# Head of a fused layernorm, state-space and feed-forward kernel: immediate epsilon, column halves, other engines for two copies, one memset moved

## Chip, core, metric

The kernel runs on one core of a Trainium2 chip. The metric is the device time of one execution in microseconds. The engines are named as in the profile: PE (TensorE, matrix multiply; PEld is its weight load), DVE (VectorE), ACT (ScalarE), POOL (GpSimd), SP (SyncE). PSUM is the memory that TensorE writes, SBUF the one that all engines work from. DMAs are issued from queues of SP, ACT and POOL.

## What is computed

x has 2048 tokens of 512 columns, all in bf16. Layernorm without weights, then two branches on the normalized tokens, and a residual:

```python
xn = (x - mean(x)) / sqrt(var(x) + 1e-5)
# branch A: diagonal complex state-space scan over the 2048 tokens, 512 states
Bu = xn @ B_bar.T;  h[t] = Lam_bar * h[t-1] + Bu[t];  yA = 2 * real(h @ C.T) + xn * Dskip
# branch B: gated feed-forward, 1376 hidden columns
yB = (silu(xn @ w_gate) * (xn @ w_up)) @ w_down
out = x + yA + yB
```

## The kernel before

Tokens are cut into 16 tiles of 128 and four chunks of 512 (four tiles each). Tokens lie on partitions in `xall`; the matrix products need columns of x on partitions, so each normalized tile is transposed into `xnT`. The order of the work is written out by hand: each engine runs its instructions in the order in which the program issues them, and a list of VectorE work (`queue`, `pump`, `need`) is fed in between matmul groups by estimated costs. Every chunk goes through gate and up products (`gateup_tile`), the product with B (`bproj_tile`, line 357), rotation, scan and rotation back on VectorE (`rotation`, lines 367 to 381; `scan`, line 399), and the output products (`out_ffn`, `out_ssm`).

The change is in the head, chunk 0, which is handled tile by tile so that TensorE can start before the whole chunk is there:

- **Loads.** Line 123 loads tile 0 on SP's queue, line 125 tile 1 on ACT's. Line 124 clears half of tile 1's place just ahead of that, so ACT's load waits for a VectorE memset. Behind them come, alternately on SP and ACT, the first two columns groups of gate (line 126, 256 KB) and up (line 127, 256 KB), tiles 2 (SP) and 3 (ACT), and the next groups of gate and up (SP). POOL loads three parameter rows and builds the identity that the transposes need.
- **Dummies.** TensorE runs nine matmuls of 512 columns on constants at once (`dummy`, line 608), and four more of 128 columns behind the transposes of tile 0.
- **Layernorm of a tile.** VectorE takes statistics (`ln_stats`, lines 185 and 186; for tiles 1 and 3 written out, lines 638 and 653), ScalarE forms 1/sqrt(var + eps) as Ln and Exp (`rstd_act`, lines 190 and 191; the Ln reads eps from a column of biases, `eps_t`), VectorE normalizes in place (`norm_dve`, line 203). In VectorE's order the statistics of tile 1 (line 638) stand between those of tile 0 and the normalization of tile 0 (line 639).
- **Transposes.** `xT_pe` transposes a tile on TensorE in two halves of two column blocks (line 220) and copies each half from PSUM to `xnT`, on VectorE (line 227) or ScalarE (line 229). For tile 0 the first half is copied by VectorE, the second by ScalarE; for tile 1 both by ScalarE; for tiles 2 and 3 both by VectorE.
- **First matmuls.** `head_mm(which, lo, hi, ks, fis)` multiplies gate (0) or up (1), tiles lo to hi, column blocks ks, hidden blocks fis (line 631). Before, the order is: gate of tile 0, both transposes of tile 1, up of tile 0, then gate and up of tile 1, and so on.

Behind the head, `table_ops` builds a cosine table `c16` and a sine table `s16` on VectorE and ScalarE (`Sin`, line 284; the cosine of each half comes after the sine). `rotation` multiplies u by both: two products with its first part (f1 with the cosine, f2 with the sine), f3 (second part with the sine), their sum f4, f5 and f6.

Of the kernel before, what the change touches and what calls it, by code (L numbers as in the profile page):

```python
# [10 lines left out]
F32 = mybir.dt.float32  # L11
BF16 = mybir.dt.bfloat16
ALU = mybir.AluOpType
ACT = mybir.ActivationFunctionType
# [9 lines left out]
def kernel(  # L24
# [17 lines left out]
    nc = tc.nc  # L42
    _, L, D = A_x.shape
# [8 lines left out]
    KD = D // 128  # L52
    NQ = Pst // 128
    FT = (F + 127) // 128
# [4 lines left out]
    LA, LB = 32, 64  # L59
    FL = (FT - 1) * 128  # L60
    assert fsz[-1] == LA + LB and NCH % 2 == 0
    EPS = 1e-5

    const = ctx.enter_context(tc.tile_pool(name="const", bufs=1))
# [8 lines left out]
    def bank(shape=(128, CW), dtype=F32):  # L73
        return psum.tile(list(shape), dtype, name="ps")

    def flat(ap3):
        return ap3.rearrange("p q j -> p (q j)")
# [7 lines left out]
    xall = const.tile([128, NT, D], BF16, name="xall")  # L85
    xnT = const.tile([128, KD, L], BF16, name="xnT")
# [9 lines left out]
    wd_sb = const.tile([128, FT, D], BF16, name="wd_sb")  # L96
# [7 lines left out]
    def wslice(groups, fi, k):  # L104
        for (a, b), t in zip(fgroups, groups):
            if a <= fi < b:
                return t[:, k, (fi - a) * 128:(fi - a) * 128 + fsz[fi]]
# [6 lines left out]

    neg_half = const.tile([128, TPC], F32, name="neg_half")
    nc.vector.memset(neg_half[:], -0.5)
    eps_t = const.tile([128, 1], F32, name="eps_t")
    nc.vector.memset(eps_t[:], EPS)

    nc.scalar.preload_act_table_set("natural_log_exp_and_others")  # L120


    nc.sync.dma_start(out=xall[:, 0, :], in_=x_v[:, 0, :])
    nc.vector.memset(xall[:, 1, 0:D // 2], 0.0)
    nc.scalar.dma_start(out=xall[:, 1, :], in_=x_v[:, 1, :])
    load_w1(nc.sync, wg_g, wg_v, 0)
# [5 lines left out]
    prm_rows = const.tile([128, 128], BF16, name="prm_rows")  # L132
# [28 lines left out]
    ident = const.tile([128, 128], BF16, name="ident")  # L161
# [4 lines left out]


    gu_last = [const.tile([128, CW], BF16, name=f"gu_last{i}") for i in range(3)]
    for t in (*(g[LB + LA:128, :] for g in gu_last), wd_sb[LB + LA:128, FT - 1, :]):
        nc.vector.memset(t, 0.0)  # L170


    stats = const.tile([128, NT, 6], F32, name="stats")
    mv = const.tile([128, NT, 2], F32, name="mv")
    ve = const.tile([128, NT], F32, name="ve")
# [5 lines left out]
    def xn_tile(c):  # L181
        return xn_end if c == NCH - 1 else xall[:, c * TPC:(c + 1) * TPC, :]

    def ln_stats(n):
        nc.vector.bn_stats(out=stats[:, n, :], in_=xall[:, n, :])  # L185
        nc.vector.bn_aggr(out=mv[:, n, :], in_=stats[:, n, :])

    def rstd_act(n):

        nc.scalar.activation(out=ve[:, n:n + 1], in_=mv[:, n, 1:2], func=ACT.Ln, bias=eps_t[:, 0:1])  # L190
        nc.scalar.activation(out=rstd[:, n:n + 1], in_=ve[:, n:n + 1], func=ACT.Exp, scale=-0.5)

    def ln_rstd(a, b):
# [4 lines left out]
        nc.vector.scalar_tensor_tensor(out=nb[:, a:b], in0=mv[:, a:b, 0], scalar=-1.0, in1=rstd[:, a:b],  # L198
                                       op0=ALU.mult, op1=ALU.mult)

    def norm_dve(n):
        c, i = divmod(n, TPC)
        nc.vector.tensor_scalar(out=xn_tile(c)[:, i, :], in0=xall[:, n, :], scalar1=mv[:, n, 0:1],
                                scalar2=rstd[:, n:n + 1], op0=ALU.subtract, op1=ALU.mult)

    def norm_act(n):
# [3 lines left out]

    HK = KD // 2

    def xT_pe(n, on_dve=(), prm_too=False):

        c, i = divmod(n, TPC)
        for h in range(2):
            tp = bank((128, HK * 128 + 128), BF16)
            for k in range(HK):
                lo = (h * HK + k) * 128
                nc.tensor.transpose(out=tp[:, k * 128:(k + 1) * 128], in_=xn_tile(c)[:, i, lo:lo + 128],  # L220
                                    identity=ident[:])
            if prm_too and h == 1:
                prm_transpose(tp[:, HK * 128:])
            dst = xnT[:, h * HK:(h + 1) * HK, n * 128:(n + 1) * 128]
            src = tp[:, 0:HK * 128].rearrange("p (k t) -> p k t", k=HK)
            if h in on_dve:
                nc.vector.tensor_copy(out=dst, in_=src)
            else:
                nc.scalar.copy(out=dst, in_=src)
        return tp[:, HK * 128:]  # L230

    def xT_dma(n):
# [12 lines left out]
    c2re, nc2re, nc2im = sm("c2re", NQ), sm("nc2re", NQ), sm("nc2im", NQ)  # L245
    kk, fs1, fc1 = sm("kk", 2, NQ), sm("fs1", 2, NQ), sm("fc1", 2, NQ)
    V = nc.vector

    def prm_transpose(pp):
        nc.tensor.transpose(out=pp, in_=prm_rows[:], identity=ident[:])  # L250

    def params_a(pp):
        V.tensor_copy(out=prm[:].rearrange("p t q -> p (t q)"), in_=pp[:, 0:3 * NQ])
# [107 lines left out]
    def rotation(src, dst, back):  # L361

        box = {}

        def mul(i, tab):
            t = ssm.tile([128, W], BF16, name="pm", bufs=3)
            V.tensor_tensor(out=t[:], in0=flat(src()[:, i]), in1=flat(tab[:]), op=ALU.mult)  # L367
            return t

        def f1():  # L370
            box[0] = mul(0, c16)
        def f2():
            box[1] = mul(0, s16)
        def f3():
            box[2] = mul(1, s16)
        def f4():
            V.tensor_tensor(out=flat(dst()[:, 0]), in0=box[0][:], in1=box[2][:], op=ALU.subtract if back else ALU.add)
        def f5():
            box[3] = mul(1, c16)
        def f6():  # L380
            V.tensor_tensor(out=flat(dst()[:, 1]), in0=box[3][:], in1=box[1][:], op=ALU.add if back else ALU.subtract)
        return [(1.15, f) for f in (f1, f2, f3, f4, f5, f6)]

    def ssm_ops(c):

# [6 lines left out]


        ops = rotation(lambda: u_tiles[c], lambda: u_tiles[c], False)
        for q in range(NQ):
            for part in range(2):
# [20 lines left out]
        def wt():  # L417
            if c not in w_tiles:
                w_tiles[c] = ssm.tile([128, 2, NQ, CW], BF16, name="wt", bufs=2)
            return w_tiles[c]  # L420
        back = rotation(g, wt, True)
        return ops, back

# [182 lines left out]
    def dummy(n, cols):  # L606
        for _ in range(n):
            nc.tensor.matmul(warm[:, 0:cols], lhsT=ones[:, 0:128], rhs=ones[:, 0:cols], start=True, stop=True)  # L608

    def ln_rest(c, on_act):  # L610
        ops = [(0.7, lambda n=n: ln_stats(n)) for n in range(c * TPC, (c + 1) * TPC)]
        def fin():
            ln_rstd(c * TPC, (c + 1) * TPC)
        def nbf():
            ln_nb(c * TPC, (c + 1) * TPC)
        ops += [(0.1, fin)]
        tail = [(0.1, nbf)] if on_act else []
        for n in range(c * TPC, (c + 1) * TPC):
            def one(n=n):
                (norm_act if on_act else norm_dve)(n)  # L620
                xT_dma(n)
            tail.append((0.05 if on_act else 0.35, one))
        return ops, tail
# [3 lines left out]
    def head_mm(which, lo, hi, ks, fis):  # L627

        for fi in fis:
            for k in ks:  # L630
                nc.tensor.matmul(held[fi][which][:, lo * 128:hi * 128], lhsT=wslice((wg_g, wu_g)[which], fi, k),  # L631
                                 rhs=xnT[:, k, lo * 128:hi * 128], start=(k == 0), stop=(k == KD - 1))

    allk = range(KD)
    dummy(9, CW)
    ln_stats(0)
    rstd_act(0)
    nc.vector.bn_stats(out=stats[:, 1, :], in_=xall[:, 1, :])
    norm_dve(0)
    nc.vector.bn_aggr(out=mv[:, 1, :], in_=stats[:, 1, :])  # L640
    rstd_act(1)
    xT_pe(0, on_dve=(0,))
    dummy(4, 128)
    norm_dve(1)
    ln_stats(2)

    head_mm(0, 0, 1, range(0, HK), (0, 1))
    head_mm(0, 0, 1, range(HK, KD), (0, 1))
    xT_pe(1)
    rstd_act(2)  # L650
    head_mm(1, 0, 1, range(0, HK), (0, 1))
    head_mm(1, 0, 1, range(HK, KD), (0, 1))
    nc.vector.bn_stats(out=stats[:, 3, :], in_=xall[:, 3, :])
    norm_dve(2)
    nc.vector.bn_aggr(out=mv[:, 3, :], in_=stats[:, 3, :])
# [3 lines left out]
    head_mm(0, 1, 2, range(HK, KD), (0, 1))  # L659
    head_mm(1, 1, 2, range(HK, KD), (0, 1))  # L660
    head_mm(0, 0, 2, allk, (2,))
    pp = xT_pe(2, on_dve=(0, 1), prm_too=True)
    head_mm(1, 0, 2, allk, (2,))
    norm_dve(3)
    params_a(pp)
    params_a2()
    head_mm(0, 2, 3, range(0, HK), range(H))
    head_mm(1, 2, 3, range(0, HK), range(H))
    xT_pe(3, on_dve=(0, 1))
    head_mm(0, 2, 3, range(HK, KD), range(H))  # L670
    head_mm(1, 2, 3, range(HK, KD), range(H))
    params_sin()
# [145 lines left out]
```

## Time and profile before

| | us |
|---|---|
| median of three runs | 179.19 |
| lowest and highest | 179.1, 179.68 |
| span of the profiled execution, first to last instruction | 177.3 |

The profiled execution is known by its span; the median of the runs is 1.9 us above it, which is what lies around the span.

| engine | busy us | share of the span |
|---|---|---|
| PE | 172.9 | 97% |
| DVE | 154.4 | 87% |
| ACT | 94.7 | 53% |
| POOL | 23.2 | 13% |

A group in the profile is a line, an engine, an operation and `out<-in`. A matmul's busy time overlaps its neighbours', since matmuls are pipelined: the distance of two starts says what one costs. `[0.44 <-DMA ...]` is idle time of the engine before the group and what ended it. The chain of work that ended last goes back from the last instruction to what released each step. The DMA view of a window names each queue with its packets in that window: q1 is SP's, q10 ACT's, q0 POOL's.

### The profile page before, as it was taken

Reading aid. Unit: us, or ns where it says so; the run is one execution under the profiler, and the core shown is the slowest. Engines: PE = TensorE matmul, PEld = TensorE weight load, DVE = VectorE, ACT = ScalarE, POOL = GpSimd, SP = SyncE. Lnnn points to the kernel's source line nnn. Section 1 sums busy time; section 2 is a strip of 40 time slices with the busy share of each in tenths; the row PEclk is TensorE's granted clock in tenths of the full one; section 3 lists DMA queues with packets and bytes.
Section 4 is the critical chain, followed back from the end, with each engine's and each line's share of the span. In section 5 each row is a group of like instructions: output and inputs, shape, how many; then the busy total and the mean of one; then the engine's idle time right before and its main releaser. Section 6 shows DMA issues by size and latency. Waiting matters only on the chain.

```text
span 177.3 us, 2449 instructions
## 1 busy us (share of the span) xinstructions
PE 172.9 (97%) x900; PEld 83.6 (47%) x916; DVE 154.4 (87%) x238; ACT 94.7 (53%) x173; POOL 23.2 (13%) x29
## 2 busy tenths in 40 slices
PE   8999999999999999999999999999999999999993
PEld 2884444444444444444444444444444444444743
DVE  6789997999999977899999999999999999990033
ACT  4589696977499369914966662013766600220000
POOL 6003000001200140000700000014280000150000
DMA  5999749973041024900440000005469500072012
GB/s 163 316 264 239 148 90 261 334 126 89 0 96 26 0 52 96 355 0 0 60 62 2 0 0 4 0 0 61 58 97 177 86 0 0 0 85 33 4 50 69
DMA packets 29131, 15.53 MB, mean 88 GB/s; under 512 B 18848, under 2 KB 29056, under 8 KB 29088
## 3 DMA queue, kind: packets, MB, share of 16 engines
q1 hardware_dynamic: 24416, 11.41, 28.8%
q0 software_dynamic: 3456, 3.28, 13.7%
q10 hardware_dynamic: 1248, 0.69, 1.3%
q8 instruction: 7, 0.11, 0.3%
q14 instruction: 4, 0.03, 0.1%
HBM read 8.03 MB, written 5.24 MB: 75 GB/s over the span
## 4 chain that ended last, share of the span: by engine, by line
PE 98%; issue 1%; DVE 0%
PE ps L432 36%; PE ps L528 19%; PE ps L545 16%; PE ps L357 16%; PE ps L631 3%; PE ps L608 2%; PE ps L483 2%; PE ps L535 2%; PE ps L472 1%; PE ps L220 1%; DVE res L548 0%; PE ps L250 0%
## 5 line engine op out<-in xcount | busy, mean ns | idle before, releaser
L432 PE MATMUL ps<-xnT,wg 128*128 128x512 bf16 x144 | 37.8, 379 | 0.4
L432 PE MATMUL ps<-xnT,wu 128*128 128x512 bf16 x145 | 37.3, 379 | 0.0
L528 PE MATMUL ps<-wd_sb,guT 128*128 128x512 bf16 (+2 forms) x177 | 36.7, 355 | 0.2
L399 DVE TENSOR_TENSOR_SCAN g<-r_t,car,u 128x512 bf16<-128x512 f32 x24 | 28.8, 1264 | 0.0
L545 PE MATMUL ps<-CF,wt 128*128 128x512 bf16 (+2 forms) x141 | 28.2, 355 | 0.2
L357 PE MATMUL ps<-xnT,BT 128*128 128x512 bf16 x126 | 28.2, 379 | 0.1
L446 ACT ACTIVATE guT<-ps 128x512 bf16<-128x512 f32 x40 | 24.6, 615 | 5.0 <-PE ps L432 5.0
L447 ACT CAST u<-ps 128x512 bf16<-128x512 f32 x40 | 24.1, 602 | 5.2 <-PE ps L432 5.1
L528 PEld LDWEIGHTS <-guT 128*128 128x128 bf16 x180 | 16.9, 98 | 18.0
L432 PEld LDWEIGHTS <-wu 128*128 128x128 bf16 x148 | 14.5, 98 | 17.5
L432 PEld LDWEIGHTS <-wg 128*128 128x128 bf16 x148 | 14.4, 98 | 17.2
L555 ACT CAST res<-ps 128x512 bf16<-128x512 f32 x12 | 6.7, 594 | 28.1 <-PE ps L545 28.1
L556 POOL DMA_DIRECT2D out_dram<-res x12 | 10.5, 1041 | 78.0 <-ACT res L555 78.0
L545 PEld LDWEIGHTS <-wt 128*128 128x128 bf16 x144 | 13.4, 98 | 14.4 <-issue 0.4
L357 PEld LDWEIGHTS <-BT 128*128 128x128 bf16 x128 | 12.5, 98 | 15.1
L359 ACT CAST u<-ps 128x512 bf16<-128x512 f32 x32 | 17.6, 588 | 3.7 <-PE ps L357 3.6
L451 DVE TENSOR_TENSOR guT<-guT,u 128x1024 bf16<-128x1024 bf16 x20 | 13.5, 680 | 0.0
L548 DVE TENSOR_TENSOR res<-ps,xn_end 128x512 bf16<-128x512 f32 (+2 forms) x6 | 3.0, 514 | 11.8 <-PE ps L545 11.8
L195 POOL TENSOR_TENSOR rstd<-ve,neg_half 128x4 f32<-128x4 f32 x3 | 5.3, 1761 | 53.9 <-DVE ve L194 53.9
L367 DVE TENSOR_TENSOR pm<-u,c 128x2048 bf16<-128x2048 bf16 x8 | 9.8, 1221 | 1.2 <-ACT c L284 1.1
L185 DVE BATCH_NORM_STATS2 stats<-xall 128x6 f32<-128x512 bf16 x14 | 9.5, 676 | 0.4 <-DMA xall<-in_A_x_dram 0.4
L367 DVE TENSOR_TENSOR pm<-g,c 128x2048 bf16<-128x2048 bf16 x8 | 9.7, 1215 | 0.1
(108 smaller groups left out, 166.6 us busy)
## 6 DMA issues: line engine op xcount, KB each, us to landing
out_dram<-in_A_x_dram SPq DMA_DIRECT2D x1, 1536.0 KB, 7.0
out_dram<-res POOLq DMA_DIRECT2D x12, 128.0 KB, 3.0
out_dram<-xall POOLq DMA_DIRECT2D x3, 512.0 KB, 7.6
wd_sb<-in_B_w_down_dram SPq DMA_DIRECT2D x1, 1280.0 KB, 10.9
xall<-in_A_x_dram SPq DMA_DIRECT2D x1, 1024.0 KB, 6.1
xall<-in_A_x_dram SPq DMA_DIRECT2D x2, 256.0 KB, 4.6
wg<-in_B_w_gate_dram SPq DMA_DIRECT2D x1, 512.0 KB, 5.6
wu<-in_B_w_up_dram SPq DMA_DIRECT2D x1, 512.0 KB, 6.1
```

Of the source, the lines that this page charges most:

```text
L185: nc.vector.bn_stats(out=stats[:, n, :], in_=xall[:, n, :])
L357: nc.tensor.matmul(ps[:], lhsT=BT[:, part, k, q * 128:(q + 1) * 128], rhs=xnT[:, k, c * CW:(c + 1) * CW], start=(k == 0), stop=(k == KD - 1))
L359: nc.scalar.copy(out=u_tiles[c][:, part, q, :], in_=ps[:])
L367: V.tensor_tensor(out=t[:], in0=flat(src()[:, i]), in1=flat(tab[:]), op=ALU.mult)
L399: V.tensor_tensor_scan(out=g()[:, part, q, :], data0=r_t[:, q:q + 1].to_broadcast([128, CW]), data1=u_tiles[c][:, part, q, :], initial=ini ...
L432: nc.tensor.matmul(ps[:fs, lo:hi], lhsT=wslice(groups, fi, k), rhs=xnT[:, k, c * CW + lo:c * CW + hi], start=(k == 0), stop=(k == KD - 1))
L446: nc.scalar.activation(out=guT[:fs, fi, :], in_=psg[:fs], func=ACT.Silu)
L447: nc.scalar.copy(out=u_pair[c][:fs, fi % 2, :], in_=psu[:fs])
L451: products.append(lambda: V.tensor_tensor(out=g, in0=g, in1=u, op=ALU.mult))
L528: nc.tensor.matmul(o[:], lhsT=gu_tiles[c][:, fi, i * 128:(i + 1) * 128], rhs=wd_sb[:, fi, lo:hi], start=(fi == 0), stop=False)
L545: nc.tensor.matmul(o[:], lhsT=w_tiles[c][:, part, q, i * 128:(i + 1) * 128], rhs=CF[:, part, q, lo:hi], start=False, stop=(c > 0 and part ...
L556: nc.gpsimd.dma_start(out=out_v[:, n, :], in_=res[:], accum_op=ALU.add)
```

## The change

- The Ln takes epsilon as an immediate; `eps_t` and its memset are gone.
- The memset of `wd_sb`'s unused rows moves from the end of the memsets to before the memset of tile 1's place (and so before ACT's first load).
- `norm_dve` can take a range of columns; tiles 0 and 1 are normalized in two halves.
- `xT_pe` handles one half. For tile 0 VectorE copies both halves, and one of the four short dummies stands between the halves. For tile 1 the first half of up of tile 0 stands between the two halves, its second half behind them; `rstd_act(2)` comes after that.
- In the forward rotation the two sine products f2 and f3 come ahead of the cosine product f1; the rotation back keeps its order.
- The calls for tiles 2 and 3 are written for the new form of `xT_pe` and do what they did.

```diff
-    eps_t = const.tile([128, 1], F32, name="eps_t")
-    nc.vector.memset(eps_t[:], EPS)
...
     nc.sync.dma_start(out=xall[:, 0, :], in_=x_v[:, 0, :])
+    nc.vector.memset(wd_sb[LB + LA:128, FT - 1, 0:D], 0.0)
     nc.vector.memset(xall[:, 1, 0:D // 2], 0.0)
     nc.scalar.dma_start(out=xall[:, 1, :], in_=x_v[:, 1, :])
...
-    for t in (*(g[LB + LA:128, :] for g in gu_last), wd_sb[LB + LA:128, FT - 1, :]):
-        nc.vector.memset(t, 0.0)
+    for g in gu_last:
+        nc.vector.memset(g[LB + LA:128, :], 0.0)
...
-        nc.scalar.activation(out=ve[:, n:n + 1], in_=mv[:, n, 1:2], func=ACT.Ln, bias=eps_t[:, 0:1])
+        nc.scalar.activation(out=ve[:, n:n + 1], in_=mv[:, n, 1:2], func=ACT.Ln, bias=EPS)
...
-    def norm_dve(n):
+    def norm_dve(n, lo=0, hi=D):
         c, i = divmod(n, TPC)
-        nc.vector.tensor_scalar(out=xn_tile(c)[:, i, :], in0=xall[:, n, :], scalar1=mv[:, n, 0:1],
+        nc.vector.tensor_scalar(out=xn_tile(c)[:, i, lo:hi], in0=xall[:, n, lo:hi], scalar1=mv[:, n, 0:1],
...
-    def xT_pe(n, on_dve=(), prm_too=False):
+    def xT_pe(n, h, on_dve, prm_too=False):
...
-        return [(1.15, f) for f in (f1, f2, f3, f4, f5, f6)]
+        return [(1.15, f) for f in ((f1, f2, f3, f4, f5, f6) if back else (f2, f3, f1, f4, f5, f6))]
...
-    norm_dve(0)
+    norm_dve(0, 0, DH)
+    norm_dve(0, DH, D)
     nc.vector.bn_aggr(out=mv[:, 1, :], in_=stats[:, 1, :])
     rstd_act(1)
-    xT_pe(0, on_dve=(0,))
-    dummy(4, 128)
-    norm_dve(1)
+    xT_pe(0, 0, True)
+    dummy(1, 128)
+    xT_pe(0, 1, True)
+    dummy(3, 128)
+    norm_dve(1, 0, DH)
+    norm_dve(1, DH, D)
     ln_stats(2)
-
-    head_mm(0, 0, 1, range(0, HK), (0, 1))
-    head_mm(0, 0, 1, range(HK, KD), (0, 1))
-    xT_pe(1)
+    head_mm(0, 0, 1, kh[0], (0, 1))
+    head_mm(0, 0, 1, kh[1], (0, 1))
+    xT_pe(1, 0, False)
+    head_mm(1, 0, 1, kh[0], (0, 1))
+    xT_pe(1, 1, False)
+    head_mm(1, 0, 1, kh[1], (0, 1))
     rstd_act(2)
-    head_mm(1, 0, 1, range(0, HK), (0, 1))
-    head_mm(1, 0, 1, range(HK, KD), (0, 1))
```

More of the change, by code (lines that the diff above doesn't have):

```diff
@@ L211 @@
     HK = KD // 2
-    def xT_pe(n, on_dve=(), prm_too=False):
+    def xT_pe(n, h, on_dve, prm_too=False):
         c, i = divmod(n, TPC)
[L216 to L229, printed above, removed]
+        tp = bank((128, HK * 128 + 128), BF16)
+        for k in range(HK):
+            lo = (h * HK + k) * 128
+            nc.tensor.transpose(out=tp[:, k * 128:(k + 1) * 128], in_=xn_tile(c)[:, i, lo:lo + 128], identity=ident[:])
+        if prm_too:
+            nc.tensor.transpose(out=tp[:, HK * 128:], in_=prm_rows[:], identity=ident[:])
+        dst = xnT[:, h * HK:(h + 1) * HK, n * 128:(n + 1) * 128]
+        src = tp[:, 0:HK * 128].rearrange("p (k t) -> p k t", k=HK)
+        if on_dve:
+            nc.vector.tensor_copy(out=dst, in_=src)
+        else:
+            nc.scalar.copy(out=dst, in_=src)
         return tp[:, HK * 128:]
@@ L247 @@
     V = nc.vector
-    def prm_transpose(pp):
-        nc.tensor.transpose(out=pp, in_=prm_rows[:], identity=ident[:])
     def params_a(pp):
@@ L634 @@
     allk = range(KD)
+    kh = (range(0, HK), range(HK, KD))
+    DH = D // 2
     dummy(9, CW)
@@ L661 @@
     head_mm(0, 0, 2, allk, (2,))
-    pp = xT_pe(2, on_dve=(0, 1), prm_too=True)
+    xT_pe(2, 0, True)
+    pp = xT_pe(2, 1, True, True)
     head_mm(1, 0, 2, allk, (2,))
@@ L668 @@
     head_mm(1, 2, 3, range(0, HK), range(H))
-    xT_pe(3, on_dve=(0, 1))
+    xT_pe(3, 0, True)
+    xT_pe(3, 1, True)
     head_mm(0, 2, 3, range(HK, KD), range(H))
```

## The prediction

> **What bounds the kernel now.** I read the chain of work that ended last first, then the timelines of the first 12 us, engine by engine, then the DMA views of short windows. The page says where the time goes:
>
> ```profile
> span 177.3 us, 2449 instructions
> ...
> PE 98%; issue 1%; DVE 0%
> ```
>
> TensorE is the chain, nearly without a break. The list of TensorE's waits agrees: its own queue names one, 0.8 us at the launch, and its weight loads name one on another engine, 0.9 us on line 203. After 12 us, weight loads and matmuls wait for nobody. So only two things move the end: how early the useful work of TensorE starts, and how dense it is until about 12 us. The stretch in question (timeline, TensorE; columns: start us, busy us, then the group):
>
> ```profile
> 3.72 1.06 PE L608 MATMUL ps<-const-bfloat16-1.0 128*128 128x512 bf16 x2
> 4.76 0.61 PE L220 MATMUL ps<-ident,xall 128*128 128x128 bf16 x4
> 5.16 0.50 PE L608 MATMUL ps<-const-bfloat16-1.0 128*128 128x128 bf16 x4
> 5.54 0.67 PE L631 MATMUL ps<-xnT,wg 128*128 128x128 bf16 x8
> 6.05 0.39 PE L220 MATMUL ps<-ident,xall 128*128 128x128 bf16 x4
> 6.27 0.61 PE L631 MATMUL ps<-xnT,wu 128*128 128x128 bf16 x8
> 6.79 0.38 PE L631 MATMUL ps<-xnT,wg 128*128 128x128 bf16 x4
> ```
>
> The nine wide dummies start 0.427 us apart, the last at 4.15, so their slots end at 4.57; the transposes of tile 0 begin at 4.76. Between 4.57 and 7 us TensorE stands still for about 0.19 (normalization), 0.04, 0.07 and 0.07 us (copies of transposes): 0.37 us in all, and no edit of this head can win more. What feeds it (timeline, VectorE):
>
> ```profile
> 0.84 0.06 DVE L118 MEMSET eps_t<- 128x1 f32 x1
> 0.90 0.17 DVE L124 MEMSET xall<- 128x128 uint32 x1
> ...
> 2.07 0.27 DVE L170 MEMSET wd_sb<- 32x256 uint32 x1
> 2.78 0.69 DVE L185 BATCH_NORM_STATS2 stats<-xall 128x6 f32<-128x512 bf16 x1 [0.44 <-DMA xall<-in_A_x_dram]
> 3.51 0.18 DVE L186 BATCH_NORM_AGGREGATE mv<-stats 128x2 f32<-128x6 f32 x1
> 3.61 0.66 DVE L638 BATCH_NORM_STATS2 stats<-xall 128x6 f32<-128x512 bf16 x1
> 4.29 0.41 DVE L203 TENSOR_SCALAR xall<-xall,mv,rstd 128x512 bf16<-128x512 bf16 x1
> ```
>
> The statistics of tile 1 (line 638) stand ahead of tile 0's normalization (line 203), and end at 4.27, just as ScalarE has tile 0's 1/sqrt ready (4.26). Whatever delays tile 1's data delays tile 0.
>
> **The change, part by part, if every load kept its place.** These are the gains.
>
> Ln with an immediate: it takes 0.29 us, the Exp beside it, which reads no column of biases, 0.20. I take 0.09 (bounds 0 and 0.09). Tile 0's 1/sqrt is ready at 4.16.
>
> Normalization in halves: a 128x512 takes 0.41; in the run of four on line 203 at 17.97 to 19.35 starts are 0.32 apart, and the 128x4 operations of lines 296 and 329 follow one another at 0.07 to 0.08. So about 0.25 of the 0.32 scales with columns: a half starts 0.19 after the one before and takes 0.28 (bounds 0.16, a 128x4 row, and 0.41, the whole). The first half would end at 4.20 + 0.28 = 4.48 instead of 4.70; but the dummies hold TensorE until 4.57, so of 0.22 only 0.19 arrive.
>
> VectorE copies both halves of tile 0 (0.29 each, against 0.37 on ScalarE): the second half is there at 5.64 instead of 5.78. What is late next is tile 1: its normalization now stands behind two copies and ends 0.2 later (6.03 against 5.81); ScalarE's copies of tile 1 follow. That up's first half stands between tile 1's two transposes hides most of it. Following it through, the first tile-1 matmul (6.79 before) comes at 6.65: a gain of 0.13, which then persists, as TensorE is dense from there on. The moved dummies cost nothing: there are four as before.
>
> Sine table first: VectorE waited 1.12 us at 28.6 for the cosine (line 284). The sine multiply can start at 28.6, but the next one needs the last cast of u, which ends at 30.15 behind the cosine on ScalarE; I count 0.7 us of VectorE time won, and nothing at the end, since TensorE doesn't wait for VectorE there. Were that cover gone, it would be worth 0.7. In later chunks u is ready long before: chunk 1's casts end at 39.3 and its rotation starts at 74.8.
>
> **What the moved memset does to the queues.** VectorE clears wd_sb (0.27) before the memset of tile 1 instead of eps_t (a slot of 0.05), so the tile-1 memset ends 0.22 later. ScalarE's queue waits for just that memset with its first load, and two more are behind it; SP's queue is not held:
>
> ```profile
> 1.10 0.41 ACTq L125 DMA_DIRECT2D xall<-in_A_x_dram  x1
> 1.53 0.46 ACTq L112 DMA_DIRECT2D wu<-in_B_w_up_dram  x1
> 2.02 0.53 ACTq L129 DMA_DIRECT2D xall<-in_A_x_dram  x1
> ```
>
> ```profile
> 0.74 0.40 SPq L123 DMA_DIRECT2D xall<-in_A_x_dram  x1
> 1.20 0.42 SPq L112 DMA_DIRECT2D wg<-in_B_w_gate_dram  x1
> 1.66 0.51 SPq L128 DMA_DIRECT2D xall<-in_A_x_dram  x1
> ```
>
> Tile 1's load goes out at 1.32 instead of 1.10, and so behind gate's first 256 KB (1.20); up's weights at 1.75, behind tile 2 (1.66); tile 3 at 2.24, beside gate's second group (2.21). Does the order matter? The DMA views of short windows say that large loads move one after another. Between 2.9 and 3.5 us, though up's load on q10 had been issued at 1.53, only q1 moved; between 3.9 and 4.3 only q10 (and two packets of q0), though tile 2 on q1 had been issued at 1.66:
>
> ```profile
> q1 hardware_dynamic: 281, 0.14, 86.4%
> ```
>
> ```profile
> q10 hardware_dynamic: 220, 0.11, 104.5%
> ```
>
> Gate's 256 KB hold the engines for about 1.05 us, from their first packets (2.55) to up's first (3.60). If they go ahead, tile 1 lands not at 1.10 + 2.0 = 3.1 but at about 4.15 (bounds: 3.33, its own delay of 0.22 alone; 4.4, the order of packets as bad as the 1.3 us that gate's load took to its last packet).
>
> Then: tile-1 statistics start at 4.19 instead of 3.61 and end at 4.85; the first half of tile 0's normalization, next in VectorE's queue, runs from 4.77 to 5.05; the transposes start at 5.10, 0.34 later than before, and TensorE idles 0.53 after its dummies. The copy comes 0.43 after that, as before (5.53 to 5.82); the first gate matmuls start at 5.88, the second four at 6.10. Tile 1 is normalized from 5.95 to 6.42, its transposes run at 6.32 and 6.65, ScalarE's copy (0.37) ends at 7.00, and the first tile-1 matmul starts at 7.05 against 6.79: **0.27 later than before**. Half of the delay is absorbed by the halves and the earlier second copy.
>
> What stands behind: up's weights, landed at 5.73 before, are needed at 6.43, which I cost at nothing. Tile 3 landed at 6.2. If gate's second group passes it (its 128 KB moved for about 1.1 us), it lands at 7.3, just what its statistics need before they hold up tile 2's normalization; I take 0.04 for this, bounds 0 and 0.35. The parameter rows and the identity on GpSimd come 0.22 later and keep over 0.4 us of slack (identity at 3.75 before).
>
> **Sum.** 0.27 + 0.04 = 0.31 us on a span of 177.3, so 177.6. Outside the span the change moves nothing; the median of the shown runs lies 1.9 above it, so 179.19 + 0.31 = **179.5**.
>
> **Rivals.**
> The loads keep their order (179.06). Up to 3.6 us the trace also fits a strict turn between the two queues, SP, ACT, SP, ACT: then tile 1 still goes second and lands at 3.34, before 3.61, and the gain of 0.13 stands, bounds 0.37 (every idle stretch gone) and a loss of 0.08 (halves as slow as wholes, 0.41). [...]
>
> The clock (slower, about 181). TensorE starts at half rate: 128-column starts are 0.107 apart until 5.38 and 0.056 after 5.54, 4.6 us after its first dummy. If a 0.53 us hole made it begin again, counted from 5.1 it would be fast only at 9.7; at most (9.7 - 5.4)/2 = 2.1 us on top of the 0.3, some 1.5 where it waits anyway. It decides if the hole is too long for whatever watches activity; the 0.19 us hole of before was not. [...]
>
> That the Ln or the halves save nothing changes little: in the forecast the Ln is hidden behind the statistics, halves at full price add 0.13.
>
> **How the numbers follow.** The order flips and costs 0.3: 0.52 (of it 0.19 beyond 0.54 us, if tile 3 or the halves add their bounds). The order holds: 0.35 (0.10 of it faster by over 0.54, which takes more than the idle I can see). The clock: 0.13. 0.3% of 179.19 is 0.54 us, about what a measurement of this kernel can tell from no change. So faster 0.10, same 0.25 + 0.33 = 0.58, slower 0.19 + 0.13 = 0.32. Range: below, the order holds with nearly all idle gone and the scatter of the runs, 178.7; above, 179.19 + 0.27 + 0.35 + 0.13 = 179.9 and some scatter, 180.1. It leaves out the clock and the extreme gains.
>
> **What would show it.** Right: VectorE's wait for tile 1 ahead of line 638's statistics, near 0.6 us; the first transposes at 5.1; TensorE without waits after 8 us. Wrong: those statistics at 3.6 and transposes at 4.57 (the order held); 128-column starts 0.107 apart after 5.6 us (the clock); any TensorE wait after 12 us, which I exclude.

## The result, and the profile after

The changed kernel takes **180.37 us** (median of six runs, 180.22 to 181.76) against 179.19: a ratio of 1.0082, 95% interval 1.0054 to 1.0111. Forecast were 179.5 us, in a range up to 180.1, so the loss came out nearly four times as large as forecast (1.18 us instead of 0.31). The six runs fall into two groups: four at 180.22 to 180.39 and two at 181.69 and 181.76. The profiled one is of the second group:

```profile
span 179.9 us, 2470 instructions
...
PE 95%; DMA 2%; ACT 0%; DVE 0%; issue 0%
```

TensorE is still the chain, but a load now has 2% of it. The head of the changed kernel in the timeline of all engines (start us, busy us, engine, line, group; idle time and its end in brackets):

```profile
0.97 0.27 DVE L122 MEMSET wd_sb<- 32x256 uint32 x1
1.20 0.42 SPq L112 DMA_DIRECT2D wg<-in_B_w_gate_dram  x1
1.31 0.17 DVE L123 MEMSET xall<- 128x128 uint32 x1
1.51 0.41 ACTq L124 DMA_DIRECT2D xall<-in_A_x_dram  x1
...
5.01 0.69 DVE L634 BATCH_NORM_STATS2 stats<-xall 128x6 f32<-128x512 bf16 x1 [1.12 <-DMA xall<-in_A_x_dram]
5.62 0.59 DVE L202 TENSOR_SCALAR xall<-xall,mv,rstd 128x256 bf16<-128x256 bf16 x2
6.01 0.39 PE L218 MATMUL ps<-ident,xall 128*128 128x128 bf16 x2 [1.23 <-DVE xall L202]
...
6.83 1.06 PE L625 MATMUL ps<-xnT,wg 128*128 128x128 bf16 x8
...
8.97 0.63 PE L625 MATMUL ps<-xnT,wg 128*128 128x128 bf16 x4
```

Read it from the top. The moved memset runs first, tile 1's load waits for the memset behind it and goes out at 1.51 (1.10 before), now behind gate's (1.20). Its data are there at 4.99 (3.12 before): VectorE stands still for 1.12 us ahead of tile 1's statistics. Tile 0's normalization, next in its queue, starts at 5.62 and the transposes at 6.01 (4.76 before), after TensorE has idled 1.23 us. The first matmul of tile 1 comes at 8.97 instead of 6.79.

One row more is needed to read that last number. Weight loads of the first matmuls, from the view of this line between 6 and 9.7 us (min, median and max in ns, then first and last start):

```profile
L625 PEld LDWEIGHTS <-wg x12: 151/151/151, 6.7 to 9.2; 128*128 128x128 bf16 x12
```

They take 151 ns each until 9.7 us and 97 behind it, and matmuls start 0.107 us apart instead of 0.056: TensorE's clock is at half rate until about 9.8 us, where by the distance of the starts it was released at 5.4 in the profile of before. That is what divides the two groups of runs, as far as the experiments can show it (one execution of each kernel has a profile).

So two things were lost: about 1.1 us in every run, by the load, and 1.4 us more in some, by the clock. The 0.13 us that the other edits were to bring isn't seen. One thing went as foreseen without moving the end: at 32.77 us VectorE waits 0.46 us for the cast of u, where it waited 1.12 for the cosine table.

### The profile page after: what moved, and what is told of

Its sections match the earlier page's. It is cut to its first block, busy times and chain, and to the rows that moved or that the text cites. A ratio compares the mean times of both kernels' runs of the same rounds, so it can differ in the third digit from the quotient of the medians.

```text
span 179.9 us, 2470 instructions
## 1 busy us (share of the span) xinstructions
PE 175.1 (97%) x916; PEld 85.0 (47%) x916; DVE 155.0 (86%) x240; ACT 94.5 (53%) x172; POOL 23.3 (13%) x29
## 4 chain that ended last, share of the span: by engine, by line
PE 95%; DMA 2%; ACT 0%; DVE 0%; issue 0%
PE ps L426 36%; PE ps L522 19%; PE ps L539 15%; PE ps L351 15%; PE ps L625 4%; DMA xall<-in_A_x_dram 2%; PE ps L529 2%; PE ps L477 2%; PE ps L466 1%; PE ps L218 1%; ACT L118 0%; PE ps L602 0%; DVE xall L202 0%; DVE res L542 0%; PE ps L220 0%
## 5 line engine op out<-in xcount | busy, mean ns | idle before, releaser
L426 PE MATMUL ps<-xnT,wu 128*128 128x512 bf16 x148 | 38.0, 379 | 0.0
L361 DVE TENSOR_TENSOR pm<-u,s 128x2048 bf16<-128x2048 bf16 x8 | 9.5, 1219 | 0.5 <-ACT u L353 0.5
```

The source lines that it names most:

```text
L426: nc.tensor.matmul(ps[:fs, lo:hi], lhsT=wslice(groups, fi, k), rhs=xnT[:, k, c * CW + lo:c * CW + hi], start=(k == 0), stop=(k == KD - 1))
```

## The experiments

All were timed beside runs of the kernel before on the same chip (medians 179.18 to 179.32). Times are us; "issued" and "landed" are those of tile 1's load in the profiled execution (landed is when the last of its 16 parts was reported), "tile 1" is the start of the first gate matmul of tile 1, "clock" when TensorE's granted clock goes up to full rate by the record in the kept trace (before and e7 have no such record; there it is when matmuls of 128 columns begin to start 0.056 apart).

| kernel | median (range, runs) | ratio, 95% interval | issued | landed | tile 1 | clock | span |
|---|---|---|---|---|---|---|---|
| before | 179.19 | | 1.10 | 3.12 | 6.79 | 5.4 | 177.3 |
| changed | 180.37 (180.22 to 181.76, 6) | 1.0082, 1.0054 to 1.0111 | 1.51 | 4.99 | 8.97 | 9.8 | 179.9 |
| e1 memset back | 179.28 (179.05 to 179.73, 11) | 1.0001, 0.9992 to 1.0009 | 1.07 | 3.21 | 6.93 | 6.0 | 177.5 |
| e2 memset alone | 180.85 (180.09 to 181.82, 6) | 1.0090, 1.006 to 1.012 | 1.51 | 5.05 | 8.00 | 4.1 | 178.6 |
| e3 twelve dummies | 180.34 (180.07 to 180.45, 5) | 1.0059, 1.0047 to 1.0071 | 1.51 | 5.03 | 8.00 | 3.7 | 178.5 |
| e4 load held | 180.95 (180.08 to 181.87, 6) | 1.0107, 1.0075 to 1.0139 | 1.46 | 4.78 | 7.75 | 4.2 | 178.3 |
| e5 tile 2 held | 181.23 (180.09 to 181.65, 6) | 1.0099, 1.0072 to 1.0126 | 1.51 | 4.71 | 8.69 | 9.9 | 179.8 |
| e6 statistics later | 180.53 (180.44 to 180.67, 5) | 1.0074, 1.0062 to 1.0086 | 1.51 | 5.01 | 8.21 | 5.1 | 178.8 |
| e7 whole tiles | 179.40 (179.12 to 179.8, 12) | 1.0012, 1.0004 to 1.002 | 1.07 | 3.48 | 7.51 | 6.3 | 178.0 |
| e8 six dummies | 180.60 (179.19 to 181.35, 12) | 1.0063, 1.0038 to 1.0088 | 1.09 | 3.35 | 7.90 | 10.1 | 179.6 |
| e9 gate held too | 180.08 (180.01 to 180.34, 6) | 1.0044, 1.0032 to 1.0056 | 1.50 | 4.82 | 7.78 | 4.8 | 178.3 |
| e10 sine first alone | 179.28 (178.97 to 179.77, 12) | 0.9999, 0.9988 to 1.0011 | 1.09 | 3.25 | 7.31 | 6.5 | 177.9 |
| e11 gate held longer | 181.12 (180.09 to 181.97, 6) | 1.0107, 1.0073 to 1.014 | 1.50 | 3.81 | 7.83 | 4.6 | 178.4 |
| e12 tile 1 on SP | 179.77 (179.46 to 180.19, 8) | 1.0026, 1.0015 to 1.0038 | 1.20 | 3.24 | 7.39 | 4.3 | 178.1 |

Compare the columns "tile 1" and "span": where the clock is at full rate by then, each adds to its value of before what the other does, to 0.2 us (e2 1.21 and 1.3; e12 0.60 and 0.8; e1 0.14 and 0.2). A delay of tile 1's first matmul goes to the end in full. The changed kernel's 2.18 becomes 2.6, as eight more matmuls start 0.05 late each before the clock is released.

### Is it the memset? (e1, e2)

e1 is the changed kernel with the moved memset back at its old place, e2 the kernel before with nothing but that move (and `eps_t`'s memset behind it, out of its way).

```diff
# e1, against the changed kernel
-    nc.vector.memset(wd_sb[LB + LA:128, FT - 1, 0:D], 0.0)
     nc.vector.memset(xall[:, 1, 0:D // 2], 0.0)
...
     for g in gu_last:
         nc.vector.memset(g[LB + LA:128, :], 0.0)
+    nc.vector.memset(wd_sb[LB + LA:128, FT - 1, 0:D], 0.0)
```

> The changed kernel with the memset of wd_sb's rows back behind the other memsets; all other edits stay. Queue theory (the moved memset lets ACT's first load fall behind gate's, and tile 1's statistics hold up tile 0 on VectorE): tile 1 lands near 3.1 us again, the statistics of line 638 start at 3.6, the first transposes at 4.57, and the gain that I worked out for the other edits shows: 179.05 us, span 177.15, between 178.8 and 179.2. Rival (the rest of the edits costs the time: halves, VectorE's copies, transposes around up): it stays at 180 or above, and the first transposes are early but tile 1's matmuls late.

```diff
# e2, against the kernel before
-    nc.vector.memset(eps_t[:], EPS)
...
+    nc.vector.memset(wd_sb[LB + LA:128, FT - 1, 0:D], 0.0)
     nc.vector.memset(xall[:, 1, 0:D // 2], 0.0)
...
     nc.vector.memset(prm_rows[:], 0.0)
+    nc.vector.memset(eps_t[:], EPS)
```

> The kernel before with that one edit: wd_sb's memset ahead of tile 1's (eps_t is cleared behind prm_rows, so that ACT's first load goes out at 1.51 as in the changed kernel). Queue theory: nearly all of the loss, 180.4 us (180.1 to 181.9), since nothing of the other edits shortens the way from tile 1's data to tile 0's transposes; tile 1's statistics wait for their load until about 5.0. Rival: 179.2 to 179.5, a delay of the load that is hidden.

e1 runs like the kernel before, e2 like the changed one. The timeline of e2, TensorE:

```profile
6.14 0.40 PE L221 MATMUL ps<-ident,xall 128*128 128x128 bf16 x4 [1.61 <-DVE xall L204]
...
8.00 0.38 PE L632 MATMUL ps<-xnT,wg 128*128 128x128 bf16 x4
```

So the memset's place is the whole of the loss, and the other edits together gain nothing that e1's interval can tell (0.13 us would be a ratio of 0.9993, just inside). In e1 they do their part at first: the transposes start at 4.67 instead of 4.76. Its timeline:

```profile
4.26 0.60 DVE L202 TENSOR_SCALAR xall<-xall,mv,rstd 128x256 bf16<-128x256 bf16 x2
...
4.67 0.40 PE L218 MATMUL ps<-ident,xall 128*128 128x128 bf16 x2
...
6.93 0.38 PE L625 MATMUL ps<-xnT,wg 128*128 128x128 bf16 x4
```

The two halves take 0.60 us together, where a whole tile takes 0.41. Of that execution's 6.93, some 0.25 is the clock: it was released at 6.0, and five of the first matmuls started 0.107 apart instead of 0.056. 6.93 less 0.25 is 6.68, near the forecast 6.65; that is worked out, not shown. In single profiles the moment of the release (5.4 in that of before, 6.5 in e10's, which has the same head) hides a gain of this size.

### Is it the hole, the load or the order? (e3, e6)

e3 fills the hole with three more wide dummies; e6 takes tile 1's statistics out of the way of tile 0, so that the hole should close from the other side.

```diff
# e3, against the changed kernel
-    dummy(9, CW)
+    dummy(12, CW)
```

> The changed kernel with twelve wide dummies instead of nine, so that TensorE is busy until 5.85 us and the hole before the transposes at 6.0 is 0.15 instead of 1.4 us. If the hole keeps the clock at half rate for one more window (until 9.8 in the profile of the changed kernel, 5.4 before): the clock rises near 5.4 in every run, the runs at 181.7 are gone, and the median is 180.0 to 180.3. If the clock rises by chance of phase whatever TensorE does: runs of both kinds remain, 180.3 and 181.7. Either way the loss from the late load stays.

```diff
# e6, against the changed kernel
-    nc.vector.bn_stats(out=stats[:, 1, :], in_=xall[:, 1, :])
     norm_dve(0, 0, DH)
     norm_dve(0, DH, D)
-    nc.vector.bn_aggr(out=mv[:, 1, :], in_=stats[:, 1, :])
-    rstd_act(1)
     xT_pe(0, 0, True)
     dummy(1, 128)
     xT_pe(0, 1, True)
     dummy(3, 128)
+    nc.vector.bn_stats(out=stats[:, 1, :], in_=xall[:, 1, :])
+    nc.vector.bn_aggr(out=mv[:, 1, :], in_=stats[:, 1, :])
+    rstd_act(1)
```

> The changed kernel, with tile 1's statistics and what follows them put behind tile 0's two copies on VectorE, so that tile 0 waits for nothing of tile 1. Queue theory, wait on VectorE: transposes of tile 0 at 4.6 to 4.8, its gate matmuls at 5.5. If the place in VectorE's order is all, the time comes back to 179.3; if tile 1's own way from the late landing at 5.0 is as long (statistics 5.6, normalized 7.4, first matmul of tile 1 near 8.0), the hole only moves from before tile 0 to before tile 1, and the time is 180.0 to 180.3. No runs at 181.7, since TensorE has no long hole before 6 us.

In e3 tile 1 lands as late (5.03) and the time of the faster group stays, but no run is near 181.7: the longer row of dummies takes away the second loss and not the first. (Five runs are few for the former: at two late runs in six, five in a row without one come up one time in eight.) In e6 tile 0 is transposed at 4.83, as before, and its gate product runs in the gap; the time, 180.53, is no better, and a little above the 180.0 to 180.3 that I had put for a hole that only moves. The timeline of e6, TensorE:

```profile
4.83 0.38 PE L218 MATMUL ps<-ident,xall 128*128 128x128 bf16 x2
...
7.46 0.28 PE L218 MATMUL ps<-ident,xall 128*128 128x128 bf16 x2 [1.26 <-DVE xall L202]
```

The hole of 1.2 us has moved behind the gate product. So VectorE's order, which I had made the means by which tile 1 holds up tile 0, is not what costs: tile 1's own way, from its landing at 5.0 over statistics, 1/sqrt and normalization, is as long. e2 and e3 together say the same of the new head: with the same landing (5.05, 5.03) and the clock at full rate before the transposes in both, the old head and the new reach tile 1's first matmul at the same 8.00.

### The clock (e8)

e8 is the kernel before with six wide dummies instead of nine: a hole ahead of the transposes, and no load touched.

```diff
-    dummy(9, CW)
+    dummy(6, CW)
```

> The kernel before with six wide dummies instead of nine: no load and no VectorE work is touched, but TensorE stands still from 3.3 to 4.76 us, 1.4 us, as long as in the changed kernel. If a hole makes the clock late: about half of the runs lie 1 to 2 us higher, near 180.5 to 181, with 128-column starts 0.107 apart until 8 us or later in them; the others at 179.2. If the hole does nothing and the late load alone matters: all runs at 179.1 to 179.7 as before.

Three of its twelve runs are at 179.19 to 179.26, as before; nine lie between 180.09 and 181.35. In the profiled one tile 1 landed at 3.35, all work was there in time, and still the matmuls crawled. The timeline of e8 (TensorE), and its view of the weight loads between 6.9 and 9.9 us:

```profile
4.94 0.61 PE L220 MATMUL ps<-ident,xall 128*128 128x128 bf16 x4 [1.45 <-DVE xall L203]
```

```profile
L631 PEld LDWEIGHTS <-wu x16: 151/151/151, 6.9 to 9.4; 128*128 128x128 bf16 x16
```

A hole alone is enough, then, made here by fewer dummies, and costs up to 2.2 us; it does so in some executions only. The length of the last dummies tells only part of what decides. Nine wide dummies run from 0.78 to 4.53 in e2, where the clock was released at 4.1, and to 4.78 in the changed kernel, where it was late: the last one took 0.38 us or 0.63. e3's twelve dummies start 0.427 us apart until 3.72 and 0.22 from there on. But e9's dummies look like the changed kernel's, and its transposes, behind a hole of 1.06 us, are fast all the same:

```profile
0.78 4.00 PE L603 MATMUL ps<-const-bfloat16-1.0 128*128 128x512 bf16 x9 [0.78 <-PEq L805]
5.84 0.28 PE L219 MATMUL ps<-ident,xall 128*128 128x128 bf16 x2 [1.06 <-DVE xall L203]
```

The clock's own record in the kept traces gives the moment of the rise (the column "clock"; the views of the head print 1.00 for it). In the changed kernel it goes up at 9.8 and stays up for 170.67 us, past the last instruction. In e3 it rose at 3.73, 2.95 us after the first dummy. In e2, e4 and e9 it rose at 4.1, 4.2 and 4.8, 3.3 to 4.0 us after the first dummy, and stayed up through holes of 1.61, 1.2 and 1.06 us. In the changed kernel, e5 and e8 a hole of 1.23, 0.9 and 1.45 us came first, and the clock rose at 9.8, 9.9 and 10.1; in the changed kernel and e8 that is 3.8 and 5.2 us after the transposes behind the hole began. So the length of the hole does not divide these executions; whether the rise came by about the start of the hole does. By their times 18 of the 30 runs of the changed kernel, e2, e4, e5 and e9, whose holes are alike, were spared the second loss (late were 2, 3, 3, 4 and 0 of six each). What sets the moment of the rise in one execution, and so which runs are spared, no run here shows.

### Why does 0.4 us at the issue become 1.9 at the landing? (e4, e5, e9, e11, e12)

The forecast had 0.22 at the issue and 1.05 at the landing. Three theories: tile 1's load must wait for what was issued ahead of it; it shares the engines with tile 2's, issued just behind it; or a load issued this late is slow whatever stands beside it. First the DMA view of the changed kernel from 2.4 to 3.4 us (packets, MB, share of the 16 engines):

```profile
q1 hardware_dynamic: 432, 0.22, 87.4%
q10 hardware_dynamic: 2, 0.00, 2.6%
```

SP's queue, with gate's weights, has the engines to itself although tile 1's load, on q10, was issued at 1.51. Its packets come from 3.35 to 4.53, beside those of tile 2 (3.59 to 4.71), and its last part is reported at 4.99.

e4 was to set the issue to 1.3: e1's order, with one more memset ahead of tile 1's load; it took longer than I had reckoned, and the load went out at 1.46.

```diff
# e4, against the changed kernel; wd_sb's memset goes back as in e1
-    nc.vector.memset(wd_sb[LB + LA:128, FT - 1, 0:D], 0.0)
+    nc.vector.memset(xall[:, 1, :], 0.0)
     nc.vector.memset(xall[:, 1, 0:D // 2], 0.0)
```

> As e1 (memset of wd_sb back), but tile 1's place is cleared in whole and then in half, so that ACT's first load goes out near 1.3 us: behind gate's (1.20), ahead of tile 2's (1.66). It is the delay that I had forecast. If loads are served in the order of issue: gate goes first, tile 1 lands at 4.1 to 4.2, first transposes at 5.1, 179.4 to 179.6 us (more where the clock is late). If the two queues take turns: tile 1 lands at 3.3, 179.05 us, as e1.

It lands at 4.78, 180.95 us: any wait put there will do, it isn't wd_sb's memset as such. But as the issue was hardly earlier than the changed kernel's, e4 leaves open where between 1.10 and 1.46 the turn is. A few of its packets (14 from 2.4 to 3.4 us) do go beside gate's there.

e5 holds tile 2's load on SP, and what SP issues behind it, until 2.68 by memsets put ahead of it, the last one on tile 2's place:

```diff
# e5, against the changed kernel; all lines with + but the memset of xall stood further down
     load_w1(nc.scalar, wu_g, wu_v, 0)
+    prm_rows = const.tile([128, 128], BF16, name="prm_rows")
+    nc.vector.memset(prm_rows[:], 0.0)
+    gu_last = [const.tile([128, CW], BF16, name=f"gu_last{i}") for i in range(3)]
+    for g in gu_last:
+        nc.vector.memset(g[LB + LA:128, :], 0.0)
+    nc.vector.memset(xall[:, 2, 0:128], 0.0)
     nc.sync.dma_start(out=xall[:, 2, :], in_=x_v[:, 2, :])
```

> The changed kernel, with tile 2's load (and SP's loads behind it) held until about 2.6 us by a memset behind the others. In the changed kernel tile 1 landed at 5.0 and not at 4.15 as I had forecast; its packets ran beside tile 2's from 3.4 to 4.4. If that sharing is the missing 0.85 us: tile 1 lands at 4.2 to 4.4, its statistics start then, the transposes at 5.2 to 5.4, and runs with an early clock are 0.6 us faster than the changed kernel's, 179.6 to 179.8. If tile 1 is late for another reason (behind gate alone, or its completion): it lands near 5.0 again, 180.3.

Tile 1 lands at 4.71, 0.28 earlier than in the changed kernel: sharing with tile 2 is at most a third of what I had missed (4.99 against 4.15), not all of it. "At most", since e4's load, issued 0.05 earlier with tile 2 in its place, landed 0.21 earlier too; four kernels with the changed kernel's issue lie between 4.99 and 5.05 (changed, e2, e3, e6). The forecast of this run, 4.2 to 4.4, failed.

The other three set the order of tile 1 and gate. In e9 SP's load of gate is held, too, by a small memset on its place, in e11 by a longer one; in e12 tile 1 goes on SP's queue behind tile 0, and gate on ScalarE's queue, held there until the memset is done, which now clears gate's place.

```diff
# e9, against the changed kernel; e11 has wg_g[0][:] instead
     nc.scalar.dma_start(out=xall[:, 1, :], in_=x_v[:, 1, :])
+    nc.vector.memset(wg_g[0][:, 0, 0:64], 0.0)
     load_w1(nc.sync, wg_g, wg_v, 0)
```

> The changed kernel, memset of wd_sb still ahead and ACT's first load still at 1.51 us, but SP's gate load held by one more memset until ACT's has gone out (about 1.6). Everything is as late as in the changed kernel or later; only the order of tile 1 and gate is that of before. If the order is the cause: tile 1 lands at 3.5 to 3.6, its statistics start by 3.7, transposes near 4.7, no late clock, 179.3 to 179.7 us (up's weights, 0.4 later, may hold TensorE near 6.5). If the 0.4 us delay of the load itself, or the memset's place on VectorE, is the cause: 180.3 with tile 1 landing near 5.

> The changed kernel with one more memset (all of gate's first group) behind ACT's first load, so that SP's load of gate goes out at about 1.95, some 0.4 us behind tile 1's (1.51) instead of 0.3 ahead of it. Theory A (the load that is issued clearly first has the engines first): tile 1 lands at 3.5 to 3.7, its statistics start by 3.75, the transposes by 4.9, gate lands near 5.0 and can hold the first gate matmuls to about 5.4; the time is 179.2 to 179.6. Rival B (tile 1's load is late whatever stands beside it, since it is issued late): it lands at 4.7 or later, the transposes start at 5.7 or later, 180.0 to 180.5, or 181 and more where the clock is late.

```diff
# e12, against the changed kernel
-    nc.vector.memset(xall[:, 1, 0:D // 2], 0.0)
-    nc.scalar.dma_start(out=xall[:, 1, :], in_=x_v[:, 1, :])
-    load_w1(nc.sync, wg_g, wg_v, 0)
+    nc.vector.memset(wg_g[0][:, 0, 0:256], 0.0)
+    nc.sync.dma_start(out=xall[:, 1, :], in_=x_v[:, 1, :])
+    load_w1(nc.scalar, wg_g, wg_v, 0)
```

> The changed kernel with tile 1's load on SP right behind tile 0's, and gate's first group as ScalarE's first load, which the memset (now of gate's first columns) holds to about 1.5; tile 1 goes out at 1.20. wd_sb's memset stays where the change put it. Theory A (order of issue): tile 1 lands at 3.2 to 3.4, its statistics start at 3.7, the transposes at 4.6 to 4.8, gate lands by 4.8, and the time is 179.0 to 179.4: what the moved memset costs is then only the load that it holds, not the memset. Rival C (tile 1 shares the engines with tile 0 on SP's queue or with gate however they are ordered): tile 1 lands at 4.2 or later and the time is 179.7 or more.

| | tile 1: issued, landed, between | gate: issued, landed, between |
|---|---|---|
| before | 1.10, 3.12, 2.02 | 1.20, 4.27, 3.07 |
| changed | 1.51, 4.99, 3.48 | 1.20, 4.36, 3.16 |
| e9 | 1.50, 4.82, 3.32 | 1.54, 5.37, 3.83 |
| e11 | 1.50, 3.81, 2.31 | 2.04, 6.59, 4.55 |
| e12 | 1.20, 3.24, 2.04 | 1.50, 5.78, 4.28 |

e9 missed its forecast: the two were issued 0.04 apart, which is no order, and their packets went side by side (from 3.2 to 4.2 us, 285 packets on q1 and 122 on q10); both were late. With 0.3 us between them, the changed kernel's rows above show one behind the other (432 packets on q1 and 2 on q10). e11 decides between order and lateness: the same issue at 1.50, now with gate clearly behind it, lands at 3.81 instead of 4.99. (It holds tile 2 back as well, which e5 puts at no more than 0.28 of these 1.18.) The timeline of e11:

```profile
3.87 0.66 DVE L635 BATCH_NORM_STATS2 stats<-xall 128x6 f32<-128x512 bf16 x1
...
6.64 0.62 PE L626 MATMUL ps<-xnT,wg 128*128 128x128 bf16 x8 [0.77 <-DMA wg<-in_B_w_gate_dram]
```

VectorE no longer waits for tile 1, and TensorE waits for gate's weights instead, so nothing is won: my forecast of 179.2 to 179.6 took gate to land near 5.0, and it landed at 6.59. e12 is the same with an earlier start, and the wait is again gate's and up's:

```profile
5.82 0.62 PE L625 MATMUL ps<-xnT,wg 128*128 128x128 bf16 x8 [0.37 <-DMA wg<-in_B_w_gate_dram]
...
6.82 0.40 PE L625 MATMUL ps<-xnT,wu 128*128 128x128 bf16 x4 [0.27 <-DMA wu<-in_B_w_up_dram]
```

Tile 1 lands at 3.24, as forecast, and the transposes start at 4.83 (forecast 4.6 to 4.8); the forecast time, 179.0 to 179.4, took gate to land by 4.8, and it landed at 5.78. The loss, 1.0026, is a third of the changed kernel's. No kernel here is faster than the one before. So tile 1's load, where it is issued clearly ahead of gate's, lands 2.0 to 2.4 us after its issue (2.4 in e7), and the one that comes behind pays. Gate paid 1.2 us more in e12 than before, though the same two tiles went ahead of it in both. This excess isn't explained by order alone. The engines' throughput in the DMA views of the first 8 us, in 40 slices of 0.2 us, of before and then of e12:

```profile
GB/s 0 0 0 0 0 0 0 0 31 251 297 348 312 218 90 177 333 330 307 292 271 306 334 371 374 370 316 290 276 264 242 274 251 246 297 338 338 358 353 333
```

```profile
GB/s 0 0 0 0 0 0 0 0 26 266 190 302 302 210 82 8 95 182 230 287 351 348 353 341 334 329 319 311 323 251 223 252 266 278 286 272 304 302 328 348
```

Before, the dip behind the first two tiles is one slice deep (90 at 2.8 us); in e12 the engines nearly stand still from 2.8 to 3.4 (82, 8, 95), though gate's load had been issued at 1.50 and tile 2's at 1.66, over a microsecond earlier. In e9 the same view has 36, 28, 51 and 79 from 2.4 to 3.2. What holds those loads in that time no run here shows.

### Halves and sine (e7, e10)

e7 is e1 with whole-tile normalization, e10 the kernel before with only the new order of the rotation.

```diff
# e7, against e1
-    norm_dve(0, 0, DH)
-    norm_dve(0, DH, D)
+    norm_dve(0)
...
-    norm_dve(1, 0, DH)
-    norm_dve(1, DH, D)
+    norm_dve(1)
```

> e1 (memset back) with tiles 0 and 1 normalized whole, as before. In the profile of the changed kernel a half takes 0.34 us and the second starts 0.25 after the first, not 0.28 and 0.19 as I had put it, so two halves take VectorE 0.6 against 0.41. If that ate the gain of e1: 0.05 to 0.15 faster than e1, 179.1 to 179.2, tile 1's first matmul near 6.75. If the halves still help tile 0 more than they hold up tile 1: 179.3 or above.

```diff
# e10, against the kernel before
-        return [(1.15, f) for f in (f1, f2, f3, f4, f5, f6)]
+        return [(1.15, f) for f in ((f1, f2, f3, f4, f5, f6) if back else (f2, f3, f1, f4, f5, f6))]
```

> The kernel before with the order of the rotation's products alone changed (both sine products ahead of the cosine one). VectorE's wait at 28.6 us (1.12) shrinks to about 0.4 and what follows it there comes 0.7 earlier; TensorE waits for none of it, so 179.2 us, within 0.1% of before. If some later stage of TensorE does hang on VectorE: 0.2 to 0.7 us faster.

I had expected whole tiles to be faster, as two halves cost 0.19 us of VectorE more. e7 is 0.12 us slower than e1 by the medians, with intervals that overlap (1.0004 to 1.0020 and 0.9992 to 1.0009); in its profile the transposes start at 4.74 (e1: 4.67), but the larger part of its 7.51 is a wait of 0.27 for up's weights, which landed at 6.89 there and at 5.73 before. The halves help a little or nothing. e10 gives the forecast nil; its rotation, in VectorE's timeline:

```profile
30.69 1.23 DVE L367 TENSOR_TENSOR pm<-u,s 128x2048 bf16<-128x2048 bf16 x1 [0.46 <-ACT u L359]
```

## Why the prediction was wrong

**The bound was right.** Only the start of useful work and its density until about 12 us moved the end: a delay of tile 1's first matmul came through in full, and in the changed kernel no wait of TensorE follows the transposes at 6.01.

**The step that failed is the landing of tile 1: "not at 1.10 + 2.0 = 3.1 but at about 4.15 (bounds: 3.33 ... 4.4)".** It landed at 4.99, 0.84 later, above the upper bound. The mechanism was right: the moved memset puts tile 1's load behind gate's, and VectorE then waits for it ahead of line 638's statistics (1.12 us, forecast near 0.6). The size was wrong in three terms:
- the issue: 1.51, not 1.32. I had added the slots of the memsets (0.22) and not the gaps between memsets on different places: the moved one starts 0.13 later than `eps_t`'s did, and tile 1's memset 0.07 behind its end;
- tile 2, issued 0.15 behind tile 1 and not 0.56 as before, shares the engines: at most 0.28 (e5);
- the rest, some 0.4, is not taken apart by any run. Part of it is seen: tile 1's packets take 1.18 us from the first to the last (0.66 before), and the last part is reported 0.46 behind the last packet (0.28 before). The upper bound came from gate's 1.3 us to its last packet and held neither. That the load was issued late is not the reason by itself: e11's, issued at 1.50, landed in 2.31.

From there the forecast's steps stand: landing to first transposes was to take 0.95 and took 1.02. "Half of the delay is absorbed by the halves and the earlier second copy" does not: the head with them and the head without reach tile 1 at the same 8.00 (e3, e2).

**The gains.** The Ln takes 0.20 instead of 0.29, as forecast, hidden. Halves were to take 0.28 and follow 0.19 apart; they take 0.33 to 0.35 and follow 0.25 to 0.27 apart, so a half costs four fifths of a whole start distance (0.32) and not three fifths. The first half still gives 0.09 (4.67 against 4.76), not 0.19. The 0.13 at tile 1 isn't excluded by e1, and not seen. The sine first is nil, with the wait that I named in place of the cosine's. That tile 3 might hold up tile 2 cost nothing seen: tile 2's normalization waits 0.57 for 1/sqrt, not for a load.

**The rivals.** "The loads keep their order" (0.35) was false: q10 moved two packets in the microsecond that gate's load held. "The clock" (0.13, about 181) was true in two of six runs, at 181.7, though not by the hole's length alone (e2's clock, up at 4.1, stayed up through 1.61 us). I took the hole to be 0.53 us and called it perhaps too long; it was 1.23, and e8 shows such a hole to be enough without any load. Its chance hung on the same mis-sized landing, and I priced the two as alternatives, while they add up: 1.1 and 1.4. With the transposes at 6.01 and not 5.10, the forecast's own sum would have been 0.31 + 0.91 = 1.22, so 180.4, and with the clock's 1.4 about 181.8.

## What to carry to other kernels

A memset that gates a load is part of the load: moving work ahead of it is priced by where the load then stands among the others, and by the gaps between the small instructions in front, not by their busy time. Where TensorE is kept busy until its first data, look at whether the clock is already released when the filler ends (the clock's record in the trace shows it, the length of the last dummies only in part); if not, a hole there can cost a second time, in some runs only (e8: nine of twelve, up to 2.2 us), so a few runs can miss it. Ask of a late first tile what its own way to the last consumer takes: rearranging the work around it (e3, e6) only moved the hole.

## What the runs showed of the hardware

- TensorE's clock went up at moments between 3.7 (e3) and 10.1 us (e8) of the profiled executions. Where it was up by about the start of a hole it stayed up through it (1.61 us in e2, 1.2 in e4, 1.06 in e9); where a hole of 0.9 to 1.45 us came first (e5, changed, e8) it went up at 9.8 to 10.1. In the changed kernel a weight load took 151 ns before the rise and 97 behind it. What sets the moment was not shown.
- Tile 1's 128 KB, issued 0.10 to 0.54 us ahead of gate's 256 KB (before, e11), landed 2.0 to 2.4 us after the issue. Gate behind it took 3.1 (before) to 3.7 (e7) when issued at 1.20 and 4.3 to 4.6 when issued at 1.50 (e12) and 2.04 (e11); tile 1 behind gate took 3.2 (e5) to 3.5 (changed, e2, e3, e6); the engines moved 28 to 79 GB/s for 0.8 us meanwhile (e9, 2.4 to 3.2). Why was not found.
- Up's first weights landed at 5.73 (before), 6.15 (e1) and 6.89 (e7) though issued at about 1.5 in each; TensorE waited 0.27 us for them in e7 and not in the other two.
- A 128x256 normalization took 0.34 us (changed), a 128x512 0.41 (before).
